# Two key or value blocks beside each set of query scores, one tile per PSUM bank, queries planned eight sessions ahead

## The chip, the cores and the metric

The kernel runs on one core of a Trainium2 chip. The metric is device time in microseconds (us), the median of several runs. TensorE does the matrix products, ScalarE (ACT) and VectorE (DVE) the elementwise work, SyncE (SP) issues the transfers; GpSimd works only at the start.

## The reference

Two layers follow each other. The first is attention through 49 "agents" for each of 4 batches of 12,480 tokens of 128 channels; the second is a feed-forward layer of width 2048 with a squared ReLU:

```python
def sm(a, b):                       # softmax of scaled scores
    s = scale * (a @ b.transpose(0, 2, 1))
    e = np.exp(s - s.max(-1, keepdims=True))
    return e / (e.sum(-1, keepdims=True) + 1e-09)
agent_v = sm(agents, k) @ v         # 49 x 128 for each batch
x = (sm(q, agents) @ agent_v).reshape(B * N, C)
h = np.maximum(x @ w_in, 0.0)
return (h * h @ w_out).astype(np.float32)
```

All data are float32. The kernel multiplies `agent_v` by `w_in` beforehand (the *tables*, 49 x 2048 for each batch), so that the first feed-forward product takes the query's softmax weights directly.

## The kernel before, in words

The 49,920 tokens are cut into 52 *query groups* of 960 tokens (`g`), 13 for each batch. A group has two halves of 480 tokens, and the 2048 hidden features are 16 chunks of 128. A *set* is 4 chunks for one half; a *session* (`s`, the loop at the end of the function) takes two sets, the first four and the last two sessions one. There are 211 sessions, and a group lasts 4 of them; group 1 starts at session 6, group 2 at 10. Batch 1 starts at session 54, batch 2 at 106, batch 3 at 158.

**The main work of a session.** `first` makes the sets' hidden features: for each set four main products (`w` with `aw_hi`) and four narrow extra ones (`x` with `aw_ex`) that carry low-order parts; the two sets' extras stand side by side between the mains. ScalarE rectifies each set out of PSUM into `r` (`rectified`) and squares both sets (`squared`). In the next session VectorE splits the squares into a high part `g_hi` (`rounded`) and two low parts `g_lo` (`rest`). In the session after that (`LAG = 2`) `second` multiplies them by the output weights, 24 products into one bank, and VectorE copies or adds that bank into `ob` (`copied_out`), which is written out when a half is done.

**PSUM.** Its eight banks are two tags, A and B, of four banks. A session's first set goes to one tag and its second set to the other, and the tags swap from session to session. Once the first set is rectified, its four banks serve the rest of the session: bank 0 for the output sum, bank 1 (`BLOCKS`) for the background, bank 2 (`ASKED`) for query scores, bank 3 (`TURNED`) for transposed query weights. In the next session the second set's products overwrite them. `GROUPS` tells which banks share one tile: banks 0 and 1 are tiles of their own, banks 2 and 3 one tile. `rectified` issues one ACTIVATE for each tile.

**The side work.** `queries(g)` prepares a group's weights: scores of 960 tokens against 49 agents (64 matmuls whose stationary tile is 32 or 24 columns wide, through `tiled`), maximum and subtraction on VectorE, exponential on ScalarE, sum, reciprocal and scaling on VectorE, a high and a low half, and then twice four transposes, each followed by a copy to `w` and small transfers to `w` and `x`. `background(b)` makes the tables of the next batch: 13 key blocks (12 of 1024 tokens, a short one of 192; each full one 64 small matmuls, a copy to `s` and a running maximum), the maxima over all of them, 13 value blocks (subtraction, exponential, 64 small matmuls, additions), the sums, and four table products. Batch 0's are made before the sessions.

**What sets the order.** TensorE, ScalarE and VectorE instructions are chained in the order in which the program issues them (`queued`). A session has the phases L, P, A1, D and A3. P lies after the first 6 of the 24 output products; A1 after the second set's rectifying and before the squares; D on VectorE between the two low parts; A3 after the squares. Each generator of side work says by its `yield` in which phase it goes on. `plan` holds for queries the session and phase of every step; with `AHEAD = 6` the scores come 6 sessions before the group's start, and a group's scores, block work and transposes fall as the lines at `plans` say: scores in 4n, transposes in 4n+3 and 4n+1. For the background, `allowed` lets an event happen in every even session, and in an odd one if fewer events are done than the elapsed share of the batch asks for.

Of the kernel before, what the change touches and what calls it, by code (L numbers as in the profile page):

```python
# [17 lines left out]
P = 128  # L18
# [7 lines left out]
SIZES = (2, 2)  # L26
LATE = (2, 1, 1)
LAG = 2
AHEAD = 6
LEAD = 6  # L30
WCH = 256
WIDE = 512
# [1 line left out]
PRE = 10  # L34
RAW = 4
CT = 32
BEGIN = 4
SPARE = 3


@with_exitstack
def agent_attention_relu2(ctx: ExitStack, tc: tile.TileContext, qT, kT, v, agT, w_in, w_out, outT):
# [115 lines left out]

    desk = {}
    BLOCKS, ASKED, TURNED = 1, 2, 3  # L160
    GROUPS = ((0, 1), (1, 1), (2, 2))

    class Banks:
        def __init__(self, tag):
# [3 lines left out]
            x = min(n, len(GROUPS) - 1)  # L168
            return self.tiles[x][:, n - GROUPS[x][0], :]

    def bank():
        if alone[0]:
            return ps_h.tile([P, 2, 512], F32, name="h")[:, 0, :]
        return desk["at"][BLOCKS]

    def query_bank(slot):
        if alone[0]:
# [25 lines left out]
                up = min(at + CT, n)  # L203
                queued(nc.tensor.matmul, nc.tensor, out[at:up, :], stationary[:, at:up], moving, start=start, stop=stop)

    def scores(b, i, kt):
        st = state.setdefault(b, {"s": []})
        _, rows, nt = blocks[i]
        sv = bank()[:rows, : nt * NA].rearrange("p (t a) -> p t a", a=NA)
        for t in range(nt):  # L210
            tiled(sv[:, t, :], kt[:, t * rows : (t + 1) * rows], ag[:, b, :])
        s = sp.tile([P, NT * NA], F32, name="s").rearrange("p (t a) -> p t a", a=NA)
        st["s"].append(s)
        if i == 0:
            st["mx"] = small.tile([P, NT, NA], F32, name="mx")
        s, mx = (x[:rows, :nt, :] for x in (s, st["mx"]))
        yield "A1", 0
        act.copy(s, sv)
        yield "D", 0
        if i == 0:  # L220
            dve.tensor_copy(mx, s)
        else:
            dve.tensor_max(mx, mx, s)

    def maxima(b):
        st = state[b]
        m1 = small.tile([P, NA], F32, name="m1")
        dve.reduce_max(m1, st["mx"].rearrange("p t a -> p a t"), axis=AX.X)
        yield "P", 1, True
        pt = bank()  # L230
        pe.transpose(pt[:NA, :P], m1, ident)
        yield "D", 0
        m2 = small.tile([NA, 1], F32, name="m2")
        dve.reduce_max(m2, pt[:NA, :P], axis=AX.X)
        dg = small.tile([NA, NA], F32, name="dg")
        dve.tensor_scalar_mul(dg, ident[:NA, :NA], m2)
        yield "P", 1, True
        pb = bank()
        pe.matmul(pb[:, :NA], ones[:NA, :], dg, start=True, stop=True)
        yield "D", 0  # L240
        st["mb"] = small.tile([P, NA], F32, name="mb")
        dve.tensor_copy(st["mb"], pb[:, :NA])
# [14 lines left out]
    def whole_sums(b):  # L257
        st = state[b]
        e1 = small.tile([P, 2, NA], F32, name="e1")
        dve.reduce_sum(e1[:, 0, :], st["mx"].rearrange("p t a -> p a t"), axis=AX.X)  # L260
        dve.tensor_copy(e1[:, 1, :], e1[:, 0, :])
        av = st["avT"] = small.tile([C, K2], F32, name="avT")
        dve.tensor_copy(av[:, :NA], st["av"])
        dve.tensor_copy(av[:, NA:], av[:, :NA])
        yield "P", 1, True
        pz = bank()
        pe.matmul(pz[:K2, :1], e1.rearrange("p h a -> p (h a)"), ones[:, :1], start=True, stop=True)
        yield "D", 0
        rl = st["rl"] = small.tile([K2, 1], F32, name="rl")
        dve.tensor_scalar_add(rl, pz[:K2, :1], 1e-9)  # L270
        dve.reciprocal(rl, rl)

    def values(b, i, vt):
        st = state[b]
        _, rows, nt = blocks[i]
        yield "D", 0, True
        es = st["mx"][:rows, :nt, :]
        e = small.tile([P, NT, NA], F32, name="d", bufs=2)[:rows, :nt, :] if i else es
        less_maximum(b, i, e, spare())
        yield "A3", 0  # L280
        act.activation(e, e, AF.Exp, scale=scale)
        yield "P", 1
        pv = bank()
        for t in range(nt):
            tiled(pv[:C, :NA], vt[:rows, t, :], e[:, t, :], start=(t == 0), stop=(t == nt - 1))
        yield "D", 0
        if i == 0:
            st["av"] = small.tile([C, NA], F32, name="av")
            dve.tensor_copy(st["av"], pv[:C, :NA])
        else:  # L290
            dve.tensor_add(st["av"], st["av"], pv[:C, :NA])
            spare().tensor_add(es, es, e)

    def tables(b):
        st = state[b]
        rl, av = st["rl"], st["avT"]
        hi = st["hi"] = aw.tile([P, FF], F32R, name="aw_hi")
        ex = st["lo"] = aw.tile([P, NCH // NQ, P], F32R, name="aw_ex")
        for n in range(FF // 512):
            yield "P", 1, True  # L300
            cs = slice(n * 512, (n + 1) * 512)
            pw = bank()
            pe.matmul(pw[:K2, :], av, win[:, cs], start=True, stop=True)
            yield "A1", 0
            act.activation(hi[:K2, cs], pw[:K2, :], AF.Copy, scale=rl)
            yield "D", 0
            lo = aw.tile([P, 512], F32R, name="aw_lo", bufs=3)[:NA, :]
            dve.scalar_tensor_tensor(
                out=lo, in0=pw[:NA, :], scalar=rl[:NA, :], in1=hi[:NA, cs].bitcast(F32),
                op0=ALU.mult, op1=ALU.subtract,  # L310
            )
            sync.dma_start(hi[K2:, cs].bitcast(F32), lo[:SP, :].bitcast(F32))
            for t in range(NQ):
                sync.dma_start(ex[t * 32 : t * 32 + NL, n, :].bitcast(F32), lo[SP:, t * P : (t + 1) * P].bitcast(F32))
# [5 lines left out]
    def queries(g):  # L320
# [23 lines left out]
        weights[g] = []  # L344
        for j in range(2):
            yield
            pt = query_bank(TURNED)
            for t in range(NT // 2):
                queued(
                    nc.tensor.matmul, nc.tensor, pt[:K2, t * TP : (t + 1) * TP], pp[:, j * (NT // 2) + t, :], identr, start=True, stop=True  # L350
                )
            if not alone[0]:
                yield
            w = qp.tile([P, G], F32R, name=f"w{j}", bufs=2)
            x = qp.tile([P, G], F32R, name=f"x{j}", bufs=2)
            act.copy(w[:K2, :], pt[:K2, :G])
            weights[g].append((w, x))
            yield
            sync.dma_start(w[K2:, :].bitcast(F32), w[:SP, :].bitcast(F32))
            for t in range(NQ):  # L360
                sync.dma_start(x[t * 32 : t * 32 + NL, :].bitcast(F32), w[SP:NA, :].bitcast(F32))
# [94 lines left out]
            nc.sync.dma_start(outT[:, t : t + G], whole[0])  # L456

    def background(b):
        kt = load_keys(b, 0, kv, "kt")
        for i in range(NK):  # L460
            yield "P", 1, True
            nxt = load_keys(b, i + 1, kv, "kt") if i + 1 < NK else load_values(b, 0, kv, "vt")
            yield from scores(b, i, kt)
            kt = nxt
        yield from maxima(b)
        vt = kt
        for i in range(NK):
            nxt = load_values(b, i + 1, kv, "vt") if i + 1 < NK else None
            yield from values(b, i, vt)
            vt = nxt  # L470
        yield from whole_sums(b)
        yield from tables(b)

    EVENTS = 2 * NK + 3 + FF // 512

    def step(gen):

# [55 lines left out]
    with tc.tile_pool(name="pre", bufs=PRE) as pre, tc.tile_pool(name="dec", bufs=2) as dec:  # L533
# [49 lines left out]
        ahead = queries(1)  # L583
        next(ahead)
        todo.update(gen=background(1), done=0, start=BEGIN)
        todo["next"] = (*next(todo["gen"]), 0)

        mx = pre.tile([P, 512], F32, name="mx0", bufs=1)
        ss = []
# [139 lines left out]
    for g in range(1, B * NB):  # L729
        gen = queries(g) if g > 1 else ahead  # L730
        u = starts[g] - AHEAD
        if g > 1:
            plans(gen, (u - 2, "L"))
        t0, t1 = u + 3, u + 5
        if g == 1:
            u, t0, t1 = 1, 4, 5
        plans(gen, (u, "P"), (u, "D"), (u, "A3"), (u + 1, "D"), (u + 1, "A3"), (u + 2, "D"))
        for t in (t0, t1):
            plans(gen, (t, "P"), (t, "A1"), (t, "A1"))

    def allowed(s):
        if s < todo["start"]:
            return False
        if s % 2 == 0:
            return True
        return todo["done"] < (s - todo["start"] + 1) * EVENTS / (todo["end"] - todo["start"] - SPARE)

    def phase(name, s):
        for gen in plan.pop((s, name), ()):
            step(gen)  # L750
        while todo["next"]:
            (at, lead, *event), since = todo["next"][:-1], todo["next"][-1]
            if at != name or s < since + lead:
                break
            if event:
                if not allowed(s if name == "P" else s + 1):
                    break
                todo["done"] += 1
            said = step(todo["gen"])
            todo["next"] = said and (*said, s)  # L760

    made, x, early = {}, None, None
    todo["end"] = starts[NB]
    for s in range(len(sessions) + LAG):
# [3 lines left out]
        if s in starts and s // 2 and starts.index(s) % NB == 0:  # L768
            assert not todo["next"]
            b = starts.index(s) // NB  # L770
            if b + 1 < B:
                todo.update(gen=background(b + 1), done=0, start=s, end=starts[(b + 1) * NB])
                todo["next"] = (*step(todo["gen"]), s)
        phase("L", s)

        tags = "AB" if s <= len(EARLY) or (s - len(EARLY)) % 2 == 0 else "BA"
# [48 lines left out]
        if s >= LAG:  # L825
            copied_out(*sessions[s - LAG], o)
        phase("A3", s)


_NAMES = ["qT", "kT", "v", "agT", "w_in", "w_out"]  # L830
# [32 lines left out]
```

## Time and profile before

| | |
|---|---|
| median of 3 runs | 1888.68 us (1887.86 to 1888.83) |
| the profiled execution's own time | 1887.94 us |
| its span, first to last instruction | 1885.8 us |
| instructions | 39,996 |
| granted TensorE clock, mean | 0.997 |
| TensorE busy | 1859.1 us (99%) |
| VectorE busy | 1715.7 us (91%) |
| ScalarE busy | 1623.9 us (86%) |
| the span before the first session | about 61 us |

Busy is the time in which an engine has at least one instruction under way; matmuls are pipelined, and so a busy TensorE is not one at its peak. Helpers record all instructions of the sessions under line 63, so rows are told apart by tile names: `A` and `B` are the PSUM tags, `out<-in` names what an instruction writes and reads.

### The profile page before, as it was taken

How to read it: one execution, taken by the hardware profiler on the slowest of the kernel's cores; microseconds unless marked ns; L12 is line 12 of the kernel's file. 1: busy time of each engine (PE TensorE's matmuls, PEld its weight loads, DVE VectorE, ACT ScalarE, POOL GpSimd, SP SyncE). 2: the span in 40 equal slices, each digit the busy share in tenths (PEclk: the TensorE clock that was granted, in tenths of full speed). 3: DMA queues.
4: the chain of work that ended last, by engine and by line, in shares of the span. 5: the costliest groups of instructions: out<-in, count | busy, mean ns of one | idle time of the engine just before them, and what ended most of it. 6: DMA issues, size and time to landing. Idle time of an engine off the chain costs nothing.

```text
span 1885.8 us, 39996 instructions
## 1 busy us (share of the span) xinstructions
PE 1859.1 (99%) x17186; PEld 1464.5 (78%) x17186; DVE 1715.7 (91%) x1487; ACT 1623.9 (86%) x1834; POOL 21.0 (1%) x24
## 2 busy tenths in 40 slices
PE   8899999999999999999999999999999999999998
PEld 4577877877778878777778787878777877877787
DVE  7799899999899899999998899999999999999997
ACT  5688888888888888888898888888888998999996
POOL 2100000000000000000000000000000000000000
PEclk9999999999999999999999999999999999999999
DMA  9222212211122222321112221322111111111100
GB/s 374 87 90 85 82 54 77 94 61 52 54 72 78 87 61 67 95 70 59 56 42 78 94 64 33 94 73 68 52 40 43 46 39 51 40 44 45 37 27 24
DMA packets 54820, 131.47 MB, mean 70 GB/s; under 512 B 6508, under 2 KB 34828, under 8 KB 54644
## 3 DMA queue, kind: packets, MB, share of 16 engines
q1 hardware_dynamic: 54644, 128.93, 21.4%
q8 instruction: 135, 2.21, 0.5%
q14 instruction: 41, 0.34, 0.1%
HBM read 80.97 MB, written 25.56 MB: 56 GB/s over the span
## 4 chain that ended last, share of the span: by engine, by line
PE 90%; DVE 8%; ACT 1%; issue 1%; POOL 0%; DVEq 0%; ACTq 0%; POOLq 0%
PE A L63 46%; PE B L63 42%; DVE g_lo L63 3%; DVE g_hi L63 2%; DVE ob L63 1%; DVE mx L63 1%; DVE z L63 1%; DVE e L63 1%; DVE t L63 0%; PE h L63 0%; ACT r L63 0%; DVE rest L63 0%; PE o L63 0%; PE psa L63 0%; DVE d L63 0%
## 5 line engine op out<-in xcount | busy, mean ns | idle before, releaser
L63 DVE TENSOR_TENSOR g_lo<-r,g_hi 128x1920 fp32r<-128x1920 f32 (+1 forms) x422 | 894.5, 2126 | 7.5
L63 ACT ACTIVATE r<-r 128x3840 f32<-128x3840 f32 (+1 forms) x217 | 719.5, 3319 | 2.2
L63 ACT ACTIVATE r<-B 128x480 f32<-128x480 f32 (+1 forms) x618 | 393.3, 723 | 132.1 <-PE B L63 132.1
L63 ACT ACTIVATE r<-A 128x480 f32<-128x480 f32 (+1 forms) x630 | 400.8, 723 | 71.4 <-PE A L63 71.4
L63 DVE CAST g_hi<-r 128x3840 fp32r<-128x3840 f32 (+1 forms) x217 | 448.6, 2067 | 1.7 <-ACT r L63 1.7
L63 PE MATMUL A<-g_hi,wo_lo 128*128 128x480 f32 x832 | 328.4, 395 | 0.0
L63 PE MATMUL B<-g_hi,wo_lo 128*128 128x480 f32 x832 | 324.9, 390 | 1.3 <-ACT r L63 0.7
L63 PE MATMUL A<-g_hi,wo_hi 128*128 128x480 f32 x832 | 317.2, 381 | 0.0
L63 PE MATMUL B<-g_hi,wo_hi 128*128 128x480 f32 x832 | 316.6, 381 | 0.0
L63 PE MATMUL A<-w,aw_hi 128*128 128x480 f32 x840 | 230.0, 395 | 3.6 <-ACT r L63 2.0
L63 PE MATMUL B<-w,aw_hi 128*128 128x480 f32 x824 | 223.8, 393 | 0.0
L63 PE MATMUL A<-g_lo,wo_hi 128*128 128x480 f32 x832 | 215.1, 380 | 0.6 <-ACT r L63 0.6
L63 PE MATMUL B<-g_lo,wo_hi 128*128 128x480 f32 x832 | 214.9, 380 | 0.6 <-ACT r L63 0.6
L63 PEld LDWEIGHTS A<-w,aw_hi 128*128 128x128 f32 x840 | 150.0, 188 | 59.5 <-issue 34.0
L63 PEld LDWEIGHTS B<-w,aw_hi 128*128 128x128 f32 x824 | 146.7, 188 | 49.8 <-issue 30.7
L63 PEld LDWEIGHTS A<-g_hi,wo_lo 128*128 128x128 f32 x832 | 156.6, 188 | 30.2 <-issue 2.4
L63 PEld LDWEIGHTS B<-g_hi,wo_lo 128*128 128x128 f32 x832 | 156.5, 188 | 27.4 <-DVE g_hi L63 1.3
L63 PEld LDWEIGHTS A<-g_hi,wo_hi 128*128 128x128 f32 x832 | 156.6, 188 | 25.6 <-issue 2.2
L63 PEld LDWEIGHTS A<-g_lo,wo_hi 128*128 128x128 f32 x832 | 156.2, 188 | 25.9 <-ACT r L63 0.9
L63 PEld LDWEIGHTS B<-g_lo,wo_hi 128*128 128x128 f32 x832 | 156.2, 188 | 25.8 <-ACT r L63 0.9
L63 PEld LDWEIGHTS B<-g_hi,wo_hi 128*128 128x128 f32 x832 | 156.3, 188 | 23.4 <-issue 0.7
L63 DVE COPY ob<-A 128x480 f32<-128x480 f32 x103 | 67.7, 657 | 61.6 <-PE A L63 58.3
(169 smaller groups left out, 1280.6 us busy)
## 6 DMA issues: line engine op xcount, KB each, us to landing
qt<-in_qT SPq DMA_DIRECT2D x52, 480.0 KB
out_T<-ob SPq DMA_DIRECT2D x104, 240.0 KB
kt<-in_kT SPq DMA_DIRECT2D x36, 512.0 KB
vt<-in_v SPq DMA_DIRECT2D x36, 512.0 KB
x<-w SPq DMA_DIRECT2D x416, 35.6 KB
ahead<-in_kT SPq DMA_DIRECT2D x12, 512.0 KB
ahead<-in_v SPq DMA_DIRECT2D x12, 512.0 KB
w<-w SPq DMA_DIRECT2D x104, 56.2 KB
```

Source lines behind the costliest of these rows:

```text
L63: ins = issue(*args, **kw)
```

## The change

`GROUPS` gets a tile for each bank, so that a set is rectified by four ACTIVATEs. `background` takes blocks in groups of one or two: two in sessions of one residue mod 4 (`s % 4 == starts[1] % 4`, which is 2), one in other even sessions if the count is behind. The second block of a group uses bank 3. Loads stay two blocks ahead and are issued in phase L of the session after a group. `AHEAD` becomes 8, so query scores fall in sessions 4n+2; their reciprocal work comes two sessions later instead of one, and the transposes fall in 4n+3 and the session after it, the second four into bank 2. Groups 1 to 3 have a table of their own (`FIRSTS`). The background begins at session 6, and its maxima, sums and tables may take any session.

```diff
-AHEAD = 6
+AHEAD = 8
-BEGIN = 4
-SPARE = 3
+BEGIN = 6
+FIRSTS = {
+    1: (0, 1, 1, 2, 2, 3, 4, 5),
+    2: (2, 4, 4, 5, 6, 7, 8, 9),
+    3: (5, 7, 7, 8, 9, 10, 11, 12),
+}
+SPARE = 9
...
-    GROUPS = ((0, 1), (1, 1), (2, 2))
+    GROUPS = ((0, 1), (1, 1), (2, 1), (3, 1))
...
-    def scores(b, i, kt):
+    def scores(b, group):
         st = state.setdefault(b, {"s": []})
...
+        outs = []
+        for (i, kt), slot in zip(group, (BLOCKS, TURNED)):
+            _, rows, nt = blocks[i]
+            sv = bank(slot)[:rows, : nt * NA].rearrange("p (t a) -> p t a", a=NA)
+            for t in range(nt):
+                tiled(sv[:, t, :], kt[:, t * rows : (t + 1) * rows], ag[:, b, :])
+            outs.append(sv)
         yield "A1", 0
...
+            act.copy(done[-1], sv)
         yield "D", 0
...
+                dve.tensor_max(mx, mx, s)
...
-    def values(b, i, vt):
+    def values(b, group):
...
+            less_maximum(b, i, es[-1], spare())
         yield "A3", 0
...
+        for e in es:
+            act.activation(e, e, AF.Exp, scale=scale)
+        yield "P", 1, "told"
+        for (i, vt), e, slot in zip(group, es, (BLOCKS, TURNED)):
...
-            pt = query_bank(TURNED)
+            pt = query_bank((TURNED, ASKED)[j])
...
+        for got, name, gate, work in ((keys, "kt", ("P", 1, "blocks"), scores), (vals, "vt", ("D", 0, "values"), values)):
+            more()
+            while used[name] < NK:
+                yield gate
+                at = used[name]
+                group = got[at : at + todo["room"]]
+                todo["done"] += len(group)
+                yield from work(b, group)
+                used[name] += len(group)
+                if used[name] < NK:
+                    yield "L", 1
+                    more()
+            if work is scores:
+                yield from maxima(b)
...
-        plans(gen, (u, "P"), (u, "D"), (u, "A3"), (u + 1, "D"), (u + 1, "A3"), (u + 2, "D"))
-        for t in (t0, t1):
+        when = FIRSTS[g] if g in FIRSTS else (u - 2, u, u, u + 2, u + 2, u + 3, u + 5, u + 6)
+        plans(gen, *zip(when[1:6], ("P", "A3", "D", "A3", "D")))
+        plan[when[1], "D"] = [*plan.get((when[1], "D"), ()), gen]
+        for t in when[6:]:
             plans(gen, (t, "P"), (t, "A1"), (t, "A1"))
...
+    def room(s):
+        if s < todo["start"]:
+            return 0
+        if s % 4 == starts[1] % 4:
+            return 2
+        late = todo["done"] < (s - todo["start"] + 1) * 2 * NK / (todo["end"] - todo["start"] - SPARE)
+        return int(late and s % 2 == 0)
+
+    def allowed(name, s, gate):
+        if gate == "told":
+            return s == todo["told"]
+        if gate == "any":
+            return s >= todo["start"]
+        if gate == "blocks":
+            todo["room"] = room(s)
+            return todo["room"] > 0
+        todo["told"] = next((t for t in range(s + 1, s + 4) if room(t)), None)
+        todo["room"] = todo["told"] and room(todo["told"])
+        return bool(todo["room"])
```

## Rows read from the trace of the kernel before

**Rows 1.** The page, part 1: busy us of each engine, share of the span, instructions.
```profile
PE 1859.1 (99%) x17186; PEld 1464.5 (78%) x17186; DVE 1715.7 (91%) x1487; ACT 1623.9 (86%) x1834; POOL 21.0 (1%) x24
```
**Rows 2.** The page, part 4: the chain that ended last, share by engine.
```profile
PE 90%; DVE 8%; ACT 1%; issue 1%; POOL 0%; DVEq 0%; ACTq 0%; POOLq 0%
```
**Rows 3.** Timeline, PE, 1443 to 1469 (start, us, engine, line, operation, tiles): session starts.
```profile
1443.17 1.03 PE L63 MATMUL A<-w,aw_hi 128*128 128x480 f32 x4
...
1450.98 1.04 PE L63 MATMUL B<-w,aw_hi 128*128 128x480 f32 x4
...
1459.19 1.03 PE L63 MATMUL A<-w,aw_hi 128*128 128x480 f32 x4
...
1468.02 1.03 PE L63 MATMUL B<-w,aw_hi 128*128 128x480 f32 x4
```
**Rows 4.** Timeline, PE, 533 to 600: session starts, and small groups of one session.
```profile
552.67 1.03 PE L63 MATMUL B<-w,aw_hi 128*128 128x480 f32 x4
...
561.84 1.03 PE L63 MATMUL A<-w,aw_hi 128*128 128x480 f32 x4
...
570.68 1.03 PE L63 MATMUL B<-w,aw_hi 128*128 128x480 f32 x4
...
579.86 1.03 PE L63 MATMUL A<-w,aw_hi 128*128 128x480 f32 x4
...
583.83 0.89 PE L63 MATMUL A<-ag,qt 128*32 128x49 f32 x64
584.55 0.88 PE L63 MATMUL A<-ag,kt 128*32 128x49 f32 x64
589.38 1.02 PE L63 MATMUL B<-w,aw_hi 128*128 128x480 f32 x4
```
**Rows 5.** Timeline, DVE, 270 to 280: from one closing add into `ob` to the next.
```profile
270.83 0.66 DVE L63 COPY ob<-A 128x480 f32<-128x480 f32 x1 [1.38 <-PE A L63]
...
275.67 0.55 DVE L63 TENSOR_REDUCE z<-e 120x8 f32<-120x392 f32 x1
...
277.18 0.56 DVE L63 TENSOR_TENSOR d<-s,mb 128x392 f32<-128x392 f32 x1
277.66 2.15 DVE L63 TENSOR_TENSOR g_lo<-r,g_hi 128x1920 fp32r<-128x1920 f32 x1
279.73 0.65 DVE L63 TENSOR_TENSOR ob<-B,ob 128x480 f32<-128x480 f32 x1
```
**Rows 6.** Timeline, PE, 270 to 290: session starts, and extras that waited.
```profile
270.63 1.03 PE L63 MATMUL B<-w,aw_hi 128*128 128x480 f32 x4
...
278.80 1.02 PE L63 MATMUL A<-w,aw_hi 128*128 128x480 f32 x4
...
280.43 0.49 PE L63 MATMUL B<-x,aw_ex 19*128 19x480 f32 x4 [0.19 <-DVE ob L63]
...
288.12 1.03 PE L63 MATMUL B<-w,aw_hi 128*128 128x480 f32 x4
```
**Rows 7.** Timeline, PE, three narrow windows: matmuls that came late.
```profile
104.17 0.49 PE L63 MATMUL B<-x,aw_ex 19*128 19x480 f32 x4 [1.80 <-DVE ob L63]
...
1255.54 0.23 PE L63 MATMUL A<-d,vt 128*32 128x49 f32 x1 [0.73 <-issue]
...
1349.40 0.49 PE L63 MATMUL A<-x,aw_ex 19*128 19x480 f32 x4 [0.53 <-DVE ob L63]
```
**Rows 8.** Groups by shape (count | busy us, mean ns | idle us before, releaser).
```profile
L63 ACT ACTIVATE r<-A 128x480 f32<-128x480 f32 x420 | 219.3, 584 | 71.4 <-PE A L63 71.4
...
L63 DVE TENSOR_REDUCE e<-mx 128x49 f32<-128x392 f32 x3 | 2.7, 886 | 0.1
```
**Rows 9.** Timeline, ACT, 1442 to 1453: rectifying, then squares, then rectifying again.
```profile
1444.64 1.90 ACT L63 ACTIVATE r<-A 128x480 f32<-128x480 f32 x3 [0.34 <-PE A L63]
...
1448.36 3.42 ACT L63 ACTIVATE r<-r 128x3840 f32<-128x3840 f32 x1
...
1452.47 1.03 ACT L63 ACTIVATE r<-B 128x480 f32<-128x480 f32 x2 [0.68 <-PE B L63]
```

More of the change, by code (lines that the diff above doesn't have):

```diff
@@ L169, in __getitem__, with bank @@
             return self.tiles[x][:, n - GROUPS[x][0], :]
-    def bank():
+    def bank(slot=BLOCKS):
         if alone[0]:
             return ps_h.tile([P, 2, 512], F32, name="h")[:, 0, :]
-        return desk["at"][BLOCKS]
+        return desk["at"][slot]
     def query_bank(slot):
@@ L204, in tiled @@
                 queued(nc.tensor.matmul, nc.tensor, out[at:up, :], stationary[:, at:up], moving, start=start, stop=stop)
-    def scores(b, i, kt):
+    def scores(b, group):
         st = state.setdefault(b, {"s": []})
[L208 to L216, printed above, removed]
-        yield "A1", 0
-        act.copy(s, sv)
-        yield "D", 0
[L220 to L223, printed above, removed]
+        outs = []
[5 more added lines that the diff above has]
+            outs.append(sv)
+        yield "A1", 0
+        done = []
+        for (i, _), sv in zip(group, outs):
+            _, rows, nt = blocks[i]
+            s = sp.tile([P, NT * NA], F32, name="s").rearrange("p (t a) -> p t a", a=NA)
+            st["s"].append(s)
+            done.append(s[:rows, :nt, :])
+            act.copy(done[-1], sv)
+        yield "D", 0
+        for (i, _), s in zip(group, done):
+            _, rows, nt = blocks[i]
+            if i == 0:
+                st["mx"] = small.tile([P, NT, NA], F32, name="mx")
+            mx = st["mx"][:rows, :nt, :]
+            if i == 0:
+                dve.tensor_copy(mx, s)
+            else:
+                dve.tensor_max(mx, mx, s)
     def maxima(b):
@@ L228, in maxima @@
         dve.reduce_max(m1, st["mx"].rearrange("p t a -> p a t"), axis=AX.X)
-        yield "P", 1, True
+        yield "P", 1, "any"
         pt = bank()
@@ L236, in maxima @@
         dve.tensor_scalar_mul(dg, ident[:NA, :NA], m2)
-        yield "P", 1, True
+        yield "P", 1, "any"
         pb = bank()
@@ L264, in whole_sums @@
         dve.tensor_copy(av[:, NA:], av[:, :NA])
-        yield "P", 1, True
+        yield "P", 1, "any"
         pz = bank()
@@ L271, in whole_sums @@
         dve.reciprocal(rl, rl)
-    def values(b, i, vt):
+    def values(b, group):
         st = state[b]
[L275 to L279, printed above, removed]
-        yield "A3", 0
[L281 to L285, printed above, removed]
-        yield "D", 0
[L287 to L292, printed above, removed]
+        es, outs = [], []
+        for i, _ in group:
+            _, rows, nt = blocks[i]
+            e = small.tile([P, NT, NA], F32, name="d", bufs=2) if i else st["mx"]
+            es.append(e[:rows, :nt, :])
+            less_maximum(b, i, es[-1], spare())
+        yield "A3", 0
+        for e in es:
+            act.activation(e, e, AF.Exp, scale=scale)
+        yield "P", 1, "told"
+        for (i, vt), e, slot in zip(group, es, (BLOCKS, TURNED)):
+            _, rows, nt = blocks[i]
+            pv = bank(slot)
+            for t in range(nt):
+                tiled(pv[:C, :NA], vt[:rows, t, :], e[:, t, :], start=(t == 0), stop=(t == nt - 1))
+            outs.append(pv)
+        yield "D", 0
+        for (i, _), pv in zip(group, outs):
+            if i == 0:
+                st["av"] = small.tile([C, NA], F32, name="av")
+                dve.tensor_copy(st["av"], pv[:C, :NA])
+            else:
+                dve.tensor_add(st["av"], st["av"], pv[:C, :NA])
+        for (i, _), e in zip(group, es):
+            if i:
+                _, rows, nt = blocks[i]
+                all_e = st["mx"][:rows, :nt, :]
+                spare().tensor_add(all_e, all_e, e)
     def tables(b):
@@ L299, in tables @@
         for n in range(FF // 512):
-            yield "P", 1, True
+            yield "P", 1, "any"
             cs = slice(n * 512, (n + 1) * 512)
@@ L458, in background, with more @@
     def background(b):
[L459 to L470, printed above, removed]
+        keys, vals = [], []
+        def more():
+            for load, got, name in ((load_keys, keys, "kt"), (load_values, vals, "vt")):
+                while len(got) < NK and len(got) < used[name] + 2:
+                    got.append((len(got), load(b, len(got), kv, name)))
+                if len(got) < NK:
+                    break
+        used = {"kt": 0, "vt": 0}
+        for got, name, gate, work in ((keys, "kt", ("P", 1, "blocks"), scores), (vals, "vt", ("D", 0, "values"), values)):
[12 more added lines that the diff above has]
+                yield from maxima(b)
         yield from whole_sums(b)
         yield from tables(b)
-    EVENTS = 2 * NK + 3 + FF // 512
     def step(gen):
@@ L585, in agent_attention_relu2 @@
         todo.update(gen=background(1), done=0, start=BEGIN)
-        todo["next"] = (*next(todo["gen"]), 0)
+        todo["next"] = (next(todo["gen"]), 0)
         mx = pre.tile([P, 512], F32, name="mx0", bufs=1)
@@ L731, in agent_attention_relu2 @@
         u = starts[g] - AHEAD
+        when = FIRSTS[g] if g in FIRSTS else (u - 2, u, u, u + 2, u + 2, u + 3, u + 5, u + 6)
         if g > 1:
[L733 to L736, printed above, removed]
-        plans(gen, (u, "P"), (u, "D"), (u, "A3"), (u + 1, "D"), (u + 1, "A3"), (u + 2, "D"))
-        for t in (t0, t1):
+            plans(gen, (when[0], "L"))
+        plans(gen, *zip(when[1:6], ("P", "A3", "D", "A3", "D")))
+        plan[when[1], "D"] = [*plan.get((when[1], "D"), ()), gen]
+        for t in when[6:]:
             plans(gen, (t, "P"), (t, "A1"), (t, "A1"))
-    def allowed(s):
+    def room(s):
         if s < todo["start"]:
[L743 to L746, printed above, removed]
+            return 0
[14 more added lines that the diff above has]
+        return bool(todo["room"])
     def phase(name, s):
@@ L751, in phase @@
         while todo["next"]:
-            (at, lead, *event), since = todo["next"][:-1], todo["next"][-1]
-            if at != name or s < since + lead:
+            (at, lead, *gate), since = todo["next"]
+            if at != name or s < since + lead or gate and not allowed(name, s, *gate):
                 break
[L755 to L758, printed above, removed]
             said = step(todo["gen"])
-            todo["next"] = said and (*said, s)
+            todo["next"] = said and (said, s)
     made, x, early = {}, None, None
@@ L772, in agent_attention_relu2 @@
                 todo.update(gen=background(b + 1), done=0, start=s, end=starts[(b + 1) * NB])
-                todo["next"] = (*step(todo["gen"]), s)
+                todo["next"] = (step(todo["gen"]), s)
         phase("L", s)
@@ L827, in agent_attention_relu2 @@
         phase("A3", s)
+    assert not plan and not todo["next"]
 _NAMES = ["qT", "kT", "v", "agT", "w_in", "w_out"]
```

## The prediction

> **What bounds the kernel now.** Read the page's busy shares first: TensorE is busy 99% of the span, VectorE 91%, ScalarE 86% [rows 1]. A busy TensorE proves little, so the chain of waits comes next: it runs through TensorE for 90% of the span and through VectorE for 8% [rows 2]. So what TensorE does in a session is the time, except where VectorE holds it up. Then read TensorE's timeline, taking the first four products of a session (MATMUL <-w,aw_hi) as its start. Late in the run, without key or value blocks, a session takes 7.81 us when it is plain, 8.21 with four transposes, 8.83 with one set of query scores (64 small matmuls, tiles of 32 columns) [rows 3]. Earlier, with blocks: transposes and a key block 9.17 and 9.18, a block alone 8.84, query scores and a block 9.52 [rows 4].
>
> These differences are the prices. Over the plain session query scores cost 1.02 us and a lone block 1.03. Over the session with query scores, a block beside them costs only 9.52 - 8.83 = 0.69; the same comes from the starts of the two groups, 584.55 - 583.83 = 0.72 [rows 4]. So 64 small matmuls cost 0.70, and going into them and back 0.33, once for a row of groups. Beside the four transposes a block costs 9.175 - 8.21 = 0.97: there the entry is still 0.27.
>
> Last, VectorE's hold. It works in order, and the add into `ob` closes its session: it frees the bank that the next session's second extras write. Session 270.63 has the reciprocal work for a query set and the subtraction for a value block between its two low halves. Its `ob` starts at 270.83, the small work at 275.67, the second low half at 277.66, the next `ob` at 279.73: 8.90 us, of which 1.99 is small work and 6.91 the rest [rows 5]. The session takes 8.17, so `ob` is 0.93 into the next one instead of 0.20, the extras wait [rows 6], and that session takes 9.32, where a lone block makes 8.84 (a value block some 0.05 more): 0.43 lost. Hence the first 0.5 us are free, and a session of length L bears about L - 6.6 of small work on VectorE. One small operation takes 0.48 there (277.18 to 277.66, [rows 5]). What exceeds it goes to TensorE at once, for `ob` can't run ahead of the products.
>
> **The change, part by part.** *Blocks beside query scores.* I walked the two planners session by session, numbers from the code: from 54 on, query scores move from 56, 60, ... to 54, 58, ..., the same sessions that take two blocks. There are 3 x 24 full blocks. Before, 27 stand beside query scores, 21 beside transposes, 24 alone. After, 50 stand beside query scores (24 pairs, two more full blocks beside short ones), 20 beside transposes (session 4n, one block when the count is behind), and two in session 6 share one entry. Lone entries fall from 24 to 1: 23 x (1.05 - 0.70) = 8.0 us; one transposes entry less, 0.3; of the six short blocks of the batches' ends four instead of one stand beside query scores, two beside transposes and none alone, about 0.6. Together 8.9 us of TensorE. The third group's price isn't in the trace: no session has three. It is at least the 0.70 of the second group's matmuls if they run as these do, and at most a lone block's 1.05 if it has its own entry; I take 0.70, since the second group had the same stationary sizes and the same kind of bank. The other end is a rival.
>
> Nothing else on TensorE changes in number: transposes move from odd sessions to 4n+3 and 4n (0.38 each), the nine matmuls for maxima, sums and tables of a batch only change sessions.
>
> *Start.* Two blocks leave sessions 4 and 5 (1.7 us of the 8.9), where VectorE sets the pace: the extras at 104.17 waited 1.80 us for `ob` [rows 7]. Session 6 has a pair instead of one (0.70 more), VectorE is about 1 us earlier for the missing maximum and copy. By session 7 this yields 0.3 us with one block fewer done, not the 1.0 that the blocks' own prices give: 0.7 is lost of the 8.9.
>
> *VectorE's load.* The whole work is the same, but put elsewhere. Gone: sessions like 270.63, where the reciprocal work stands beside a subtraction under 8.17 us; there are six such losses of 0.43, 2.5 us. New: value singles are told for session 4n, pairs for 4n+2, so the plain session 4n+1 gets the query's low half and two subtractions: 3 x 0.48 = 1.44 against 7.81 - 6.6 = 1.2, 0.2 lost in each of ten sessions, 2.2. Twice reciprocal work and two subtractions stand in a session of 8.7 with the maxima (2.55 against 2.1): 0.9. Once the first reduction of the maxima (as long as that of the sums, [rows 8]) falls on transposes and a short block: 0.45. The sums at a batch's end cost three times about 0.69 now (the 0.53 wait at 1349.40 and the extras' own delay, [rows 7]). They are a reduction of 0.89 [rows 8] and three small copies, an estimated 1.35 in all; after, two fall into a session with a pair, which bears 3.1 of about 3.3, one stands beside transposes, which bear 2.0 of some 3.0: 1.3 for 2.1. And one gap of 0.73 within a value block at 1255.54, for which nothing is late [rows 7], I don't repeat: its session is 1.0 too long. In all 4.9 new against 5.6 gone: 0.7 less.
>
> *The pair's own session.* 9.52 + 0.70 = 10.2 us bears 3.6 of small work. Key pair: query maximum and subtraction, two maxima, 4 x 0.48 = 1.9; value pair: two small additions more, at most 2.9. But they also wait. Query scores start 3.97 us into a session [rows 4], so the third group ends near 6.1, its copy by ScalarE near 6.8, its maximum 7.3, the second low half 9.45; `ob` is due at 10.4. Hidden, with 1 us to spare and 0.5 free.
>
> *Each bank its own tile.* The rectifying of a set becomes four ACTIVATEs of 480 columns in place of 480, 480 and 960, 416 more. The row for three is 1.90 us, two take 1.03 [rows 9], one 0.584 [rows 8], so each following one adds 0.45 and four would take 1.92: 0.02 more, at most 0.17 if they did not overlap at all. Two sets in a session: 0.04 to 0.34 of ScalarE. It begins a session 1.47 us after the products (1444.64 against 1443.17, [rows 3, 9]) when that set is done; where it is ahead it only waits less, and I cost it at nothing. The cover is thinnest in session 4n+1 with two exponentials: 3.72 for two sets and 3.42 for the squares [rows 9], 0.04 more, and about 0.5 each for the exponentials make 8.2 against 7.81. It would be 0.4 late once per cycle of four sessions, and the session after it, which waits 0.2 for `ob` anyway, has the longest to catch up; I cost that at nothing too.
>
> Here the Trainium skill speaks against the change: the page ScalarE: Activation LUTs, in its section on what ACT_TABLE_LOAD costs, gives an ACTIVATE with immediates 186 ns plus 0.833 a column and lets two overlap by about 93, so an added one costs about 93 ns. The trace agrees with the single (0.584), and shows more overlap, 0.134. By the page the cover of session 4n+1 would be gone and some 0.1 us be lost in ten sessions: 1 us on the sum.
>
> What bank tiles free: reads of the scores bank no longer hold writes to the transposes bank. The sessions of [rows 3, 4] repeat to 0.05 us, which leaves no such wait in them, so I give it nothing.
>
> *Loads.* Blocks are asked for at the start of a session, two at a time, at least one whole session (8 us) before use, on the same queue. Nothing in the steady sessions waited for one; nothing is added.
>
> Sum: 8.9 - 0.7 + 0.7 = 8.9 us off the profiled execution's 1887.94: 1879.0. The median of the runs, 1888.68, stands 0.74 above that execution, so I forecast **1879.5**; with the uncertain waits (each term within a factor of two) 1876 to 1884.
>
> **The rivals.** *A. The third group pays its own entry.* Then the 8.0 us of the lone entries and most of the 0.6 stay: about 1888, no change. Against it: the second group of a row paid none [rows 4].
>
> *B. Pairs bunch the work until VectorE ends the session.* If in the 27 sessions with a pair the closing `ob` comes late, TensorE stands still before the extras as at 280.43 [rows 6], and the loss repeats per pair. From 0.33 us in each it eats the gain, from 0.47 the kernel is slower by more than can be missed; at 0.55, about the copy of one more block, 1879.5 + 15 = 1894.5. It decides where the pair's small work ends 1.5 us later than I work out, plus that. For it: VectorE is at 91% [rows 1] and can't run ahead; against it: the pair's session is the longest, and 1.5 us must first be used up.
>
> *C. The waits go too.* If sessions 4n+1 bear their 1.44 and the start runs 1 to 2 us freer with separate tiles, 4 us more: 1875.5.
>
> **How the numbers follow.** Forecast 64%, A 12%, B 11%, C 13%. What can be told from no change is 0.2%, 3.8 us. Faster: the forecast's nearly whole share and C, 0.77; same: most of A and a tail of the forecast, 0.12; slower: B, 0.11. The range 1874 to 1887 leaves out B and most of A.
>
> **What would show it.** TensorE's timeline: three small groups in a row, starting 0.70 to 0.72 apart, in a session of 10.2 (A: 10.5; B: the session after a pair 0.3 or more longer, extras waiting for `ob`). Sessions 4n+2 after two subtractions 0.2 longer, with a short wait for `ob`. Four rectifying ACTIVATEs in about 1.92. Plain, transposes and query sessions keep 7.81, 8.2 and 8.83; were they longer, the bank tiles would cost what I left at nothing, and the prediction would be wrong by 200 times that.

## The result, and the profile after

The changed kernel takes 1903.78 us (median of 4 runs, 1900.19 to 1907.49) against 1888.72 for the one before: a ratio of 1.0081, 95% interval 1.0058 to 1.0103. It is slower by 15 us, where 9 us less were forecast. The profiled execution took 1905.9 us, its span 1903.9.

The page of the changed kernel, part 1 (busy us, share of the span, instructions) and part 4 (shares of the chain of waits), to hold against [rows 1, 2]:

```profile
PE 1859.2 (98%) x17186; PEld 1469.1 (77%) x17186; DVE 1722.5 (90%) x1487; ACT 1650.8 (87%) x2250; POOL 20.6 (1%) x24
...
PE 91%; DVE 6%; issue 1%; ACT 1%; DMA 0%; SPq 0%; POOL 0%; DVEq 0%; POOLq 0%; ACTq 0%
```

TensorE works exactly as long as before (1859.1), in a span that is 18 us longer. The chain's part on VectorE has shrunk, and "issue" has grown from a first line of 0.7 us to this one, of the view of waits (us in total, times, longest):

```profile
PE A L68 <- issue: 18.0, 15, 2.0
```

So TensorE stood still 15 times, up to 2 us, while nothing that the profile shows was late. The timeline tells where. Below are two pair sessions of the changed kernel on TensorE, the first as forecast, the second not (start, us, engine, line, operation, tiles, count, idle time before it):

```profile
639.79 1.03 PE L68 MATMUL A<-w,aw_hi 128*128 128x480 f32 x4
...
643.76 0.90 PE L68 MATMUL A<-ag,qt 128*32 128x49 f32 x64
644.48 1.57 PE L68 MATMUL A<-ag,kt 128*32 128x49 f32 x128
...
650.01 1.02 PE L68 MATMUL B<-w,aw_hi 128*128 128x480 f32 x4
```

```profile
423.53 1.03 PE L68 MATMUL A<-w,aw_hi 128*128 128x480 f32 x4
...
427.74 0.89 PE L68 MATMUL A<-ag,qt 128*32 128x49 f32 x64
428.46 1.32 PE L68 MATMUL A<-d,vt 128*32 128x49 f32 x101
431.48 0.54 PE L68 MATMUL A<-d,vt 128*32 128x49 f32 x27 [1.70 <-issue]
...
433.27 0.60 PE L68 MATMUL A<-g_hi,wo_hi 128*128 128x480 f32 x1
433.67 0.60 PE L68 MATMUL A<-g_hi,wo_lo 128*128 128x480 f32 x1
```

The first (session 66) lasts 10.22 us: two groups after the query scores, no wait. In the second (session 42) the row of small matmuls breaks off after 64 + 101 of them and goes on 1.7 us later; it lasts 14.03. Something else follows the gap there: products that are shown with 0.60 us each and start 0.40 apart; elsewhere it is 0.38, and 0.22 apart (rows of session 78 below). By windows (stretch, length, busy us and instructions of PE, PEld, DVE, ACT and POOL, granted clock, DMA share, GB/s):

```profile
423.50:431.50 8.00, 6.30 (x192) 4.68 (x191) 6.78 (x7) 7.97 (x12) 0.00 (x0) 1.00 0.30 96
431.50:437.50 6.00, 6.00 (x45) 5.06 (x45) 3.31 (x4) 1.34 (x2) 0.00 (x0) 0.72 0.30 104
639.80:650.00 10.20, 10.20 (x233) 8.30 (x232) 9.12 (x8) 9.10 (x13) 0.00 (x0) 1.00 0.47 147
```

The granted clock is 1.00 before the gap and 0.72 on average after it: part of that stretch runs at 1.2 GHz, the lower of the two levels, and it costs another 1.7 us. Of the ten long sessions this shows in two (42 and 142).

All 24 full pairs, session by session: 14 last 10.2 to 11.2 us, ten last 11.7 to 14.3. What they have above 10.24 adds up to 28.4 us: about 20.3 are gaps within the rows and 3.3 the lower clock; of the rest 2.5 are waits of some 0.25 for `ob` in ten sessions, and 1.3 the same stop just behind the row in four. Without it the profiled execution would have taken 1877.5, near the 1879.0 that the sum gave.

VectorE was not late in the pair's own session. Its rows in session 66 (same columns):

```profile
645.02 0.56 DVE L68 TENSOR_REDUCE m<-A 120x8 f32<-120x392 f32 x1
...
646.10 1.23 DVE L68 TENSOR_TENSOR mx<-mx,s 128x392 f32<-128x392 f32 x2
647.25 2.15 DVE L68 TENSOR_TENSOR g_lo<-r,g_hi 128x1920 fp32r<-128x1920 f32 x1
650.21 0.66 DVE L68 COPY ob<-A 128x480 f32<-128x480 f32 x1 [0.82 <-PE A L68]
```

Its second low half ends 9.6 us into the session (9.45 forecast), and then it waits 0.82 for TensorE.

**Which rows break off.** I counted TensorE's instructions (weight loads, matmuls and 217 that only wait for a semaphore or set one) from the start of the program. A row of three groups has 384 of them. Take the count at the row's start modulo 256, and the place of the gap within the row:

```
session             78   142   130    18    70    42    58    30   122   110    82   134    10    34
count mod 256       54    66    71    96   113   117   117   121   130   134   137   154   184   205
matmuls to gap       -   191   189   176   167   165   165   163   159   157   155   147   132   122
start to start, ns   -  2159  1841  2179  1638  1904  1412  1903  1896  1830  1894   573   517   374
```

Count plus twice the matmuls (each with its load) is 447 to 449 in every column that has a gap. The last line is the time from the start of the matmul before the gap to the start of the one after it, usually about 0.01 us; the idle time in the rows of the profile is 0.2 less, since that matmul is shown with 0.2. A row that begins below 65 ends before 448 and never stops inside. From 66 to 137 it stops for 1.4 to 2.2 us, from 154 on for less, and at 221 and 238 not at all.

The place counts, not the kind of matmul. In session 78 the row ends at 54 + 2 x 192 = 438, five ordinary products bring the count to 448, and the sixth waits:

```profile
752.79 0.38 PE L68 MATMUL A<-g_hi,wo_hi 128*128 128x480 f32 x1
753.01 0.38 PE L68 MATMUL A<-g_hi,wo_lo 128*128 128x480 f32 x1
753.78 0.38 PE L68 MATMUL A<-g_hi,wo_hi 128*128 128x480 f32 x1 [0.39 <-issue]
```

And 256 instructions are what one packet of TensorE's instruction queue carries: part 3 of the page (packets, MB, share of 16 engines' span) has

```profile
q8 instruction: 135, 2.21, 0.5%
```

that is 16,384 bytes each, and 34,589 instructions counted / 135 = 256. (Three kernels below have other counts, and 160, 150 and 104 packets for 41,114, 38,426 and 26,581 instructions.) The packet's own records agree. For session 42:

```
packet 33 starts 428.99 us, takes 0.97; TensorE has begun 33 x 256 + 347 instructions
          ends   429.96                 33 x 256 + 449
matmuls go on    431.48                 1.5 us after the packet's end
```

In the ten long sessions the packet ended when TensorE had already begun 256n + 449; in the kernel before never later than 256n + 398. After every stop TensorE goes on 1.2 to 1.6 us after the packet's end.

### The profile page after: what moved, and what is told of

Same layout as the page of the kernel before. It is cut to its first block, busy times and chain, and to the rows that moved or that the text cites. A ratio compares the mean times of both kernels' runs of the same rounds, so it can differ in the third digit from the quotient of the medians.

```text
span 1903.9 us, 40454 instructions
## 1 busy us (share of the span) xinstructions
PE 1859.2 (98%) x17186; PEld 1469.1 (77%) x17186; DVE 1722.5 (90%) x1487; ACT 1650.8 (87%) x2250; POOL 20.6 (1%) x24
## 4 chain that ended last, share of the span: by engine, by line
PE 91%; DVE 6%; issue 1%; ACT 1%; DMA 0%; SPq 0%; POOL 0%; DVEq 0%; POOLq 0%; ACTq 0%
PE A L68 48%; PE B L68 43%; DVE g_lo L68 2%; DVE g_hi L68 1%; DVE mx L68 1%; DVE t L68 1%; ACT r L68 1%; DVE ob L68 1%; DMA ahead<-in_kT 0%; DVE z L68 0%; DVE e L68 0%; DVE rest L68 0%; PE h L68 0%; DVE m L68 0%; SPq L68 0%
## 5 line engine op out<-in xcount | busy, mean ns | idle before, releaser
L68 ACT ACTIVATE r<-B 128x480 f32<-128x480 f32 x824 | 407.0, 599 | 122.0 <-PE B L68 120.7
L68 ACT ACTIVATE r<-A 128x480 f32<-128x480 f32 x840 | 414.8, 599 | 64.7 <-PE A L68 64.4
L68 DVE TENSOR_TENSOR ob<-B,ob 128x480 f32<-128x480 f32 x105 | 68.9, 656 | 62.8 <-PE B L68 62.3
```

The costliest lines, as they stand in the source:

```text
L68: ins = issue(*args, **kw)
```

## The experiments

The theory (S): TensorE runs out of instructions. 64 small matmuls are 128 instructions in 0.70 us, and a row of three groups uses 384 faster than they are brought. Rivals: VectorE and ScalarE bunched by the pair (V), something about the third group's bank (K), the tile for each bank with its 416 more ACTIVATEs (T). Line 63 stands for the sessions' instructions in kernels made from the one before, line 68 in those made from the changed one.

**The tiles alone**, in the kernel before:

```diff
-    GROUPS = ((0, 1), (1, 1), (2, 2))
+    GROUPS = ((0, 1), (1, 1), (2, 1), (3, 1))
```

> The kernel before with one edit: each PSUM bank its own tile, so 416 more rectifying ACTIVATEs. Theory S (instruction supply: TensorE's instructions arrive in packets of 16,384 bytes, 256 instructions; a row of three groups, 384 instructions in 2.1 us, can use up what is there, and the next packet takes longer than that): nothing changes on TensorE, 1888.7 within 2 us. Rival T (the added ACTIVATEs or the finer tiles cost the time): most of the 15 us, about 1900 or more.

1888.90 against 1888.42, ratio 1.0002 (0.9992 to 1.0011): T falls. ScalarE's busy time rose from 1623.9 to 1648.4 and cost nothing. The one gap of the kernel before [rows 7] is still there, in the same session, and a second of 0.28 us has come up in session 40:

```profile
1252.34 0.89 PE L63 MATMUL A<-d,vt 128*32 128x49 f32 x62
1254.04 0.25 PE L63 MATMUL A<-d,vt 128*32 128x49 f32 x2 [0.82 <-issue]
```

This row of two groups begins at 196: 196 + 2 x (64 + 62) = 448.

**Three groups without a pair**, in the kernel before: the query scores are computed twice into the same bank. No copy, no maximum and no bank is added.

```diff
-        for t in range(NT):
-            tiled(sv[:, t, :], qt[:, t * TP : (t + 1) * TP], ag[:, b, :])
+        for _ in range(1 if alone[0] else 2):
+            for t in range(NT):
+                tiled(sv[:, t, :], qt[:, t * TP : (t + 1) * TP], ag[:, b, :])
```

> The kernel before with each set of query scores in the sessions computed twice into the same bank, one right after the other: 51 x 64 matmuls more and nothing more for ScalarE, VectorE, the transfers or the other banks. 27 sessions then have three groups in a row, the others with query scores two. Theory S: 51 x 0.70 = 36 us for the matmuls and in about 11 of the 27 a gap of 1.4 to 2.2 us in the third group, some 20 us: 1940 to 1948, gaps in rows of three alone. Rival V (VectorE or ScalarE bunched by two blocks) and rival K (writing the third group's bank beside reads of the others): no gaps, 1924.

1949.79, ratio 1.0322 (1.0303 to 1.0342): 61 us more, above V's and K's 1924 and 2 us above S's upper end. One of the ten rows that stopped for 1.3 us or more, on TensorE:

```profile
556.63 1.03 PE L63 MATMUL A<-w,aw_hi 128*128 128x480 f32 x4
...
560.60 1.59 PE L63 MATMUL A<-ag,qt 128*32 128x49 f32 x128
562.01 0.86 PE L63 MATMUL A<-ag,kt 128*32 128x49 f32 x59
564.80 0.28 PE L63 MATMUL A<-ag,kt 128*32 128x49 f32 x5 [1.93 <-issue]
```

The row begins at 74, and 74 + 2 x 187 = 448. So a row of three stops without a pair, at the same place of the stream. The ten began at 74 to 158; rows of three that began at 15 to 51 or 218 to 252 did not stop. Not only rows of three stop, as was expected: two rows of two that begin at 194 and 195 do so for 0.33 us just before their end.

**The stream shifted by half a packet**: 64 short matmuls more before the sessions of the changed kernel, nothing else.

```diff
     idled(ps_a, (512,) * 7 + (G,) * 4)
+    idled(ps_a, (16,) * 64)
```

> The changed kernel with 64 short matmuls (128 TensorE instructions, half a packet) more at its very start, where TensorE waits for keys anyway; the sessions are the same. Theory S: the gaps move to the rows that now begin between 66 and 154 instructions into a packet. The ten sessions with gaps of 1.2 us or more (18, 30, 42, 58, 70, 82, 110, 122, 130, 142) lose them, and 14, 66, 38, 62, 34, 114, 86, 138 get gaps of 1 to 2 us; the time 1893 to 1905. Rivals V and K: the same ten sessions stay long, 1903.

The gaps moved. The ten long sessions now last 10.2 to 10.7 us, and ten others stop for 1.1 to 2.3, the eight that were named among them. TensorE in session 14, which had been 10.24, and in session 42, which had been 14.03:

```profile
189.54 0.90 PE L68 MATMUL A<-ag,qt 128*32 128x49 f32 x64
190.26 1.21 PE L68 MATMUL A<-ag,kt 128*32 128x49 f32 x90
193.11 0.63 PE L68 MATMUL A<-ag,kt 128*32 128x49 f32 x38 [1.65 <-issue]
...
442.06 0.89 PE L68 MATMUL A<-ag,qt 128*32 128x49 f32 x64
442.78 1.64 PE L68 MATMUL A<-d,vt 128*32 128x49 f32 x128
...
448.38 1.02 PE L68 MATMUL B<-w,aw_hi 128*128 128x480 f32 x4
```

Session 14 begins at 140 now: 140 + 2 x 154 = 448. What a pair, a bank or a neighbour does was not changed, so this takes K and V out as causes of the gaps. The time was missed: 1916.72, ratio 1.0146 (1.0124 to 1.0168), above the 1893 to 1905 expected. Session 6 began at 109.16 instead of 95.90, and without these 13.3 us the time would be 1903.5. I had not counted what the added matmuls do to the start: they keep TensorE busy up to 17.50 us, where the products for the keys had begun at 6.44, and the granted clock of the first 20 us is 0.72 instead of 1.00.

**Pairs beside the transposes**: never three groups in a row.

```diff
         if s % 4 == starts[1] % 4:
-            return 2
+            return 1
...
-        return int(late and s % 2 == 0)
+        return 2 * int(late and s % 2 == 0)
```

> The changed kernel with one block beside query scores and pairs in sessions 4n, beside four transposes, when the count is behind: rows of two groups (256 or 264 instructions), as many pairs as before (23), nearly as few entries. Theory S: no gaps, at most one as in the kernel before; 1877 to 1883. Rival V (pairs bunch VectorE): the sessions with pairs stay 1 us too long in the mean, 1900. Rival K: about 1900 too, since the second block still goes into bank 3.

1877.41, ratio 0.9939 (0.9924 to 0.9954), no gap in any row. In its session 8 two uses share bank 3 and one overwrites the other; the next kernel has a single block there:

```diff
-        return 2 * int(late and s % 2 == 0)
+        return (2 if s > 8 else 1) * int(late and s % 2 == 0)
```

> As e4, with one block instead of two in session 8 (where e4's second block and group 2's first transposes share bank 3, so that e4's output there isn't the reference's). Theory S: as e4, no gap over 1 us in any row, 1877 within 2 us, faster than the kernel before by 0.5 to 0.7%. Rival V: pairs beside transposes give back their entries as `ob` waits, 1885 or more.

**1878.05 (1877.89 to 1879.92), ratio 0.9944 (0.9930 to 0.9957): faster than both kernels.** TensorE, a pair beside transposes and a block beside query scores:

```profile
576.58 1.02 PE L68 MATMUL A<-w,aw_hi 128*128 128x480 f32 x4
...
580.46 0.48 PE L68 MATMUL A<-identr,pp 120*98 120x120 f32 x4
580.87 1.60 PE L68 MATMUL A<-ag,kt 128*32 128x49 f32 x128
...
586.44 1.03 PE L68 MATMUL B<-w,aw_hi 128*128 128x480 f32 x4
...
594.26 1.04 PE L68 MATMUL A<-w,aw_hi 128*128 128x480 f32 x4
...
598.24 0.90 PE L68 MATMUL A<-ag,qt 128*32 128x49 f32 x64
598.95 0.87 PE L68 MATMUL A<-ag,kt 128*32 128x49 f32 x64
```

Pairs are still made, in 9.86 us. From session 6 to 54 this kernel takes 428.3 us (the changed one 437.3), in the next two batches 454.0 and 453.9 (461.5, 465.6), from 158 to 206 396.5 (396.2).

**The same with the old tiles:**

```diff
-    GROUPS = ((0, 1), (1, 1), (2, 1), (3, 1))
+    GROUPS = ((0, 1), (1, 1), (2, 2))
```

> As e5, with the tiles of the kernel before (banks 2 and 3 one tile, three ACTIVATEs a set). Theory S: the tiles have no part in it, 1878 within 2 us. Rival F (finer tiles are what lets a block write bank 3 while bank 2 is still read): the pairs beside transposes wait, 1 us in each of 23 sessions, about 1900.

1878.76, ratio 0.9947 (0.9931 to 0.9964): the tiles have no part in the gain either.

**A pause before the third group**: 12 of the session's output products go between the pair's two blocks in the changed kernel (the last lines stand in `scores` and in `values`; `desk["work"]` is the session's `second`).

```diff
+    def paused():
+        for _ in range(12):
+            next(desk["work"], None)
...
+            if slot == TURNED:
+                paused()
```

> The changed kernel with 12 of the session's output products (24 instructions, 2.6 us) put between the second and the third group of each row; the same instructions in all. Theory S: the next packet arrives in the pause, gaps over 1 us go (28 us of excess in pair sessions), the third group pays an entry of 0.33 in 25 sessions: 1884 to 1890. Rivals V and K: VectorE's and ScalarE's work for the third group comes 2.6 us later still, so the loss stays or grows: 1903 or more.

The gaps went, and the time did not follow: 1934.26, ratio 1.0240 (1.0226 to 1.0254), where S wanted at most 1890. TensorE:

```profile
575.18 1.03 PE L68 MATMUL A<-w,aw_hi 128*128 128x480 f32 x4
...
579.87 0.88 PE L68 MATMUL A<-ag,kt 128*32 128x49 f32 x64
...
583.48 0.90 PE L68 MATMUL A<-ag,kt 128*32 128x49 f32 x64
...
585.74 1.03 PE L68 MATMUL B<-w,aw_hi 128*128 128x480 f32 x4
...
588.23 0.48 PE L68 MATMUL A<-x,aw_ex 19*128 19x480 f32 x4 [1.04 <-DVE ob L68]
```

The pair's session is 10.56 at best, its own entry of 0.33 above 10.22. But its third group ends 2.9 us later, and with it the copy and the maximum, the second low half and `ob`; the next session's extras wait 1.03 to 1.31 in 22 of 24 cases, and that session takes 9.5 to 9.8 in 20 of them instead of 8.2 (twice 11.3, with a part at 1.2 GHz). This is rival B, made by the pause. The time is on the side that V and K named (1903 or more); but the gaps, which they don't explain, went as S said. The pause is no remedy.

**Rows of two to six**, in the kernel before: the query scores of groups 42 to 51 are repeated in place.

```diff
-        for t in range(NT):
-            tiled(sv[:, t, :], qt[:, t * TP : (t + 1) * TP], ag[:, b, :])
+        for _ in range((g - 38) // 2 if g > 40 else 1):
+            for t in range(NT):
+                tiled(sv[:, t, :], qt[:, t * TP : (t + 1) * TP], ag[:, b, :])
```

> The kernel before with the query scores of groups 42 to 51 repeated in place, late in the run where no blocks stand: rows of 2, 2, 3, 3, 4, 4, 5, 5, 6, 6 groups of 128 instructions. Theory S: rows of 1 and 2 take 0.70 a group; from 4 groups on every row has a gap near 2 us, and the longest have two, so that in a long row TensorE gets 256 instructions in some 3 to 4 us instead of 1.4. Rivals V and K: 0.70 a group throughout.

One run: 1939.43. Of the two rows of three one stops (2.12 us, it begins at 99), and behind the other, which begins at 54, an ordinary product waits 1.08 us at the same count. Rows of four stop once (1.94 and 1.91 us), rows of five and six twice. Session 196, a row of six that begins at 85:

```profile
1794.61 2.20 PE L63 MATMUL A<-ag,qt 128*32 128x49 f32 x182
1798.83 2.59 PE L63 MATMUL A<-ag,qt 128*24 128x49 f32 x128 [2.02 <-issue]
1802.57 1.83 PE L63 MATMUL A<-ag,qt 128*24 128x49 f32 x74 [1.15 <-issue]
```

85 + 2 x 182 = 449, and the second stop comes just 128 matmuls, 256 instructions, later. From one resumption to the next it is 1802.57 - 1798.83 = 3.74 us here, and 3.47, 3.47 and 4.02 in the other three rows that stop twice: over a long row the supply is 256 instructions in 3.5 to 4.0 us, where the matmuls alone need 1.4.

**Half the instructions**: stationary tiles twice as wide in the changed kernel, so that a row of three has 192 instructions instead of 384.

```diff
-            for at in range(0, n, CT):
-                up = min(at + CT, n)
+            for at in range(0, n, 2 * CT):
+                up = min(at + 2 * CT, n)
```

> The changed kernel with stationary tiles 64 columns wide in `tiled` instead of 32: half the instructions for the same products, three groups are 192. Theory S: no gap over 0.5 us in any row. A group takes between 0.70 (if the streaming of 49 columns sets it) and 1.4 us (if the weight loads do); 125 groups make 1879 to 1966 us. Rivals V and K: the pair sessions lose what they lose now, above the longer groups.

No gap in any row, in pairs that are otherwise unchanged; TensorE:

```profile
565.96 1.03 PE L68 MATMUL A<-w,aw_hi 128*128 128x480 f32 x4
...
569.93 1.07 PE L68 MATMUL A<-ag,qt 128*64 128x49 f32 x31
...
570.88 2.05 PE L68 MATMUL A<-ag,kt 128*64 128x49 f32 x63
...
576.92 1.03 PE L68 MATMUL B<-w,aw_hi 128*128 128x480 f32 x4
```

But a group now takes 0.94 instead of 0.70, and for some 125 full groups that is 30 us: 1908.57, ratio 1.0105 (1.0091 to 1.0118), near the 1878 + 30 that this gives. Fewer instructions at the old speed would be the remedy, wider tiles are not.

## Why the prediction was wrong, point by point

**The failed step is the third group's price**: "at least the 0.70 of the second group's matmuls if they run as these do … I take 0.70". Both of its bounds, 0.70 and 1.05, count only the matmuls and the entry into the row; that the instructions might not be there in time was no term of it. The price is 0.70 in the rows that end before 448, and 0.70 plus a stop of 1.4 to 2.2 us in ten of 24. With the shorter stops and the lower clock that followed two of them this made some 25 of the 28.4 us, where the sum had nothing. The second error is the one that hid the first: the gap of 0.73 at 1255.54, "for which nothing is late", I did not repeat. It was the mechanism in the trace of before: a row of two groups that begins at 195 reaches 448 with its last matmul. A gap in the middle of equal, independent matmuls, with no releaser, should have been explained before a longer row was priced at its rate.

**What held.** Plain sessions, sessions with transposes, with query scores and with transposes and a block keep 7.81, 8.2, 8.84 and 9.16, with one exception: late in the run, where the session before a plain one now has the reciprocal work, the plain one takes 7.88 to 7.92 (7.85 to 7.87 with the old tiles), and the time from session 158 on is 0.9 longer than before. A pair without a stop in its row is 10.22 to 10.60 where 10.2 was worked out, and 10.82 and 10.84 in two sessions with the longer stops behind the row. Where two subtractions precede, `ob` comes about 0.25 late (0.2 forecast). Four rectifyings take, on ScalarE:

```profile
641.26 1.96 ACT L68 ACTIVATE r<-A 128x480 f32<-128x480 f32 x4 [0.54 <-PE A L68]
```

1.96 for 1.92, and the tiles alone moved nothing. The Trainium skill (ScalarE: Activation LUTs, its section on what ACT_TABLE_LOAD costs), weighed in the prediction, would by its overlap put the four at an estimated 2.06. The trace shows more overlap. The loss of 1 us that the page's figure meant is less than the ratio 1.0002 (0.9992 to 1.0011) can show; but sessions 4n+1 between pairs of value blocks, where 0.1 each would have been lost, keep 7.81.

**The start** was better than forecast: session 7 begins at 110.33 instead of 111.83, 1.5 us where 0.3 was given; rival C had named 1 to 2. (The sum itself ends at 1879.04 + 0.74 = 1879.8; 1879.5 is a slip.)

**The rivals.** A: no; a third group without a stop costs 0.70, not 1.05. B: the sign, with twice its price per pair (28.4 / 24 = 1.2 where 0.55 was taken), but not its mechanism: its own condition, VectorE 1.5 us later than worked out, is met only by the pause, and then it costs what B says it does and more. C: its start came, its other half did not, since `ob` is 0.25 late after two subtractions. None of the cases held the cause.

**The gain was real.** With the same blocks placed so that no row has three groups, the kernel takes 1878.05, 1.5 below the forecast, 10.9 (0.56%) below the kernel before. One row of blocks stands alone there, as in the changed kernel, where 24 did before; so the lone entries are worth about what the sum said, and the rows of three took this and 15 us more.

**What stays open.** That TensorE ran dry is shown by the place of the stops (in the sessions of the eleven kernels TensorE has 58 idle times of over 0.15 us with no releaser, in six of the kernels, and all end at 447 to 449, 54 of them inside rows of small matmuls and four just behind; a shift of the stream moved them), by their going when a row has fewer instructions or a pause, and by the packets' times. What makes a packet be asked for, and whether other transfers delay it, was not tried; the records show only that in the sessions of no kernel a packet n started before 256n + 150. Nor was why the clock fell after two of ten stops, and not after the others.

## What to carry to other kernels

Price a run of short instructions by its count as well as its time: here 384 instructions in 2.1 us were too many in most places of the stream, 256 in 1.4 us in almost none. An idle time with no releaser inside a row of equal instructions may be a limit of supply: count the instructions to it from the start of the program. And spread dense rows among work with longer instructions: two rows of two cost the same entries as a row of three and one of one.

## What the runs showed of the hardware

- TensorE's instructions come in packets of 16,384 bytes, 256 instructions. With packets counted from 0, it stops after about 256n + 448 instructions if packet n came too late, and goes on 1.2 to 1.6 us after that packet's transfer ends (58 stops in six kernels).
- The page of the changed kernel lists these 135 packets under q8. The Trainium skill (DMA: Bandwidth & Descriptors, section Queues, rings and completion order) puts refills in row 14. If the profile's numbers are these rows, the trace differs for TensorE: the profile has 45 instruction packets there as well (`q14 instruction: 45, 0.37, 0.1%`), nearly all of 8,192 bytes, but the ones that TensorE waited for are those of q8.
- A stop can cost twice: in two of ten sessions the granted clock, at 2.4 GHz up to the stop, fell to 1.2 GHz after it, for 1.7 us more.
- Going into rows of 32-column tiles costs 0.33 once for a row: the pause, which adds one such entry, made the pair's session 10.56 instead of 10.22 (session 66).
